# A planned attention and feed-forward kernel under another set of ranks, splits and transfer times

## Chip, core and metric

One core of a Trainium2 chip runs the kernel. The metric is device microseconds (us) for one execution, the median of several runs. Before: 872.32 us, median of 3 runs (871.31 to 877.17).

## What is computed

```python
q_pool = q.reshape(B, H, S // 2, 2, D).mean(axis=3)       # B,H,S,D = 4,8,1152,64
scores = matmul(q_pool, k.T) / sqrt(D)                    # 576 x 1152 per head
scores = scores - max(scores, axis=-1)
attn   = exp(scores) / (sum(exp(scores)) + 1e-9)
x      = matmul(attn, v)                                  # heads side by side: 2304 x 512
h      = x @ w_in                                         # 512 -> 2048
out    = (max(h, 0) + alpha * min(h, 0)) @ w_out          # 2048 -> 512
```

## The kernel before

Everything is float32; TensorE takes float32r operands (a rounded high part), and a low part is made by a subtraction, so that several products together give the precision that is wanted.

**Attention.** 32 heads run one after the other, each in stages that overlap with those of its neighbours. Preparation of head n loads the doubled transposed keys (`kk`, SP queue, L684) and the pooled queries (`qs`: for early heads two halves that are added, L680; from head 4 on a load L662 and an accumulating DMA from the GpSimd queue, L667). ScalarE makes the high parts `k1` (L694) and `q1` (L689). VectorE or GpSimd subtracts to get the low parts (keys L709, queries L722; for head 0 L806 and L796). SP copies the two halves of `k1` into `k3` (L649, two DMAs), which one pair of matmuls reads (L875) for the row maxima of the first 64 queries; the other maxima come from the pairs of L894, and VectorE reduces both from PSUM (L884, L910). The maxima are combined (L922), turned on TensorE (L928) and written by a DMA into the query operand (L944). A head then has 18 score tiles (9 key chunks, 2 query halves; matmuls L966 and L967), each followed by an exponential on ScalarE (L979) into a tile `pa`. The weighted sums with v (L1007, "AV" below) come in groups of chunks (`GROUPS`). The `pa` tiles of a head are added on VectorE or GpSimd (L992; `ADDS` names the chunks whose addition VectorE makes) into partial sums (`PARTS`: four per head before head `JH`, two from there on). For a pair of heads TensorE sums the partials over the partitions (L1029); the sums go through DRAM (`rsd` L1044, `rc` L1045, `rrd` L1050, `r` L1059), VectorE normalizes (L1066, L1078), and four DMAs store the result `xs` (L1088).

**Feed-forward.** Weights arrive as 64-bit floats and are rebuilt on VectorE and ScalarE (`wraw` L395, L398 to L419, L380, L383). Eight low sweeps (the first 5 of 16 weight blocks, during and after the last heads) and five high sweeps (the other 11) are matmuls of L471.

**Order.** A planner (`Scheduler`, lines 104 to 218) simulates five engines and the DMA queue while the program is built, and emits each operation when its simulated engine takes it. Among what can start within a slack it takes the smallest rank (`prio`), which is the head number plus or minus a constant, for example `n - KL` for the key load and `n - KS` for L709. `DF` is the fixed time in ns that it reckons for a transfer after its bytes, `D0` the same for the first loads; `TO_PE` and `FROM_PE` are its signalling times. Each engine and the SP queue then run in exactly the order written, so an SP row that waits holds back all rows behind it. Ring sizes bound how far loads run ahead (two `kk` buffers, two for pooled queries). Fillers (L1137) are matmuls on ones that keep TensorE's clock up until the simulated time `WE`; they write the PSUM bank that the AV groups use.

Of the kernel before, what the change touches and what calls it, by code (L numbers as in the profile page):

```python
# [219 lines left out]
def attention_ffn(  # L220
# [7 lines left out]
    q0: bass.AP,  # L228
    out: bass.AP,
    NLO: int = 5,  # L230
    PB: int = 14,
    QB: int = 2,
    DF: int = 1713,
    D0: int = 1171.677,
    AQ: int = 0,
    F0: float = 1.51,
    F2: float = 2.12,
    FD: tuple = (1, 1, 0),
    WE: float = 11.307,
    WG: int = 1,  # L240
    WT: float = 6.848,
    WM: int = 1,
    WB: int = 300,
    WN: int = 4,
    TO_PE: int = 164,
    FROM_PE: int = 6,
    SLP: int = 37,
    SLA: int = 171,
    SLD: int = 40,
    QL: float = -0.025,  # L250
    KL: float = 1.864,
    KR: float = 1.387,
    KS: float = -0.601,
    M0: float = 1.047,
    E0: float = 0.482,
    BD: int = 4,
    SD: tuple = (2, 16),
    LD: tuple = (0, 33),
    TD: tuple = (0, 33),
    SR: float = 0.47,  # L260
    Q0: float = -1.805,
    Q1: float = 4.468,
    GROUPS: tuple = ((3, 8), (8,)),
    PARTS: tuple = (((0, 1, 2), (3, 4), (5, 6), (7, 8)), ((0, 1, 2, 3), (4, 5, 6, 7, 8))),
    JH: int = 8,
    AB: int = 8,
    ADDS: tuple = ((2, 7, 8), (2, 7, 8)),
    PL: int = 2,
    LV: int = -9,
    LW: int = -9,  # L270
    GSB: int = 1,
    YSB: int = 4,
    R0: float = 6.415,
    R1: float = -3.03,
    R2: float = 3.013,
    R3: float = -1.183,
    W0: float = 4.578,
    W1: float = 3.204,
    W2: float = 24.069,
    W3: float = -2.969,  # L280
    YL: float = 0.328,
    MS: float = 0.123,
    EARLY: tuple = ((0, 1, 2), (3, 5), ()),
    LATE: tuple = ((0, 1, 2), (3, 5), (0, 1, 2, 3, 5)),
    SWITCH: int = 11,
    GL: float = 11.249,
    COL: float = 0.256,
    HW: float = -0.368,
    XB: int = 4,
    PT: int = 17,  # L290
    VB: int = 2,
    K1B: int = 3,
    Q1B: int = 3,
    AVB: int = 4,
# [1 line left out]
    QA: float = 1.0,  # L296
    REUSE: int = 6,
    NW: tuple = (464, 460, 460, 460, 460),
    RP: float = 32.195,
    RS: float = 0.808,  # L300
    RM: int = 31,
    RATE: float = 385.825,
):
    nc = tc.nc
# [941 lines left out]
```

## Time and profile before

| | us |
|---|---|
| median of 3 runs | 872.32 |
| the profiled execution | 870.35 |
| its span | 868.6 |
| TensorE busy | 842.8 (97%) |
| VectorE busy | 584.4 (67%) |
| ScalarE busy | 498.1 (57%) |
| GpSimd busy | 194.3 (22%) |

The page's shares are means over two unlike stages. Up to about 475 us the heads run: VectorE is busy for nine tenths of that time and TensorE has short gaps. After it the feed-forward runs, TensorE has no gap to speak of and VectorE is at a quarter for most of the time. What a change of order is worth has therefore to be read from the first stage.

### The profile page before, as it was taken

How to read it: one execution, taken by the hardware profiler on the slowest of the kernel's cores; microseconds unless marked ns; L12 is line 12 of the kernel's file. 1: busy time of each engine (PE TensorE's matmuls, PEld its weight loads, DVE VectorE, ACT ScalarE, POOL GpSimd, SP SyncE). 2: the span in 40 equal slices, each digit the busy share in tenths (PEclk: the TensorE clock that was granted, in tenths of full speed). 3: DMA queues.
4: the chain of work that ended last, by engine and by line, in shares of the span. 5: the costliest groups of instructions: out<-in, count | busy, mean ns of one | idle time of the engine just before them, and what ended most of it. 6: DMA issues, size and time to landing. Idle time of an engine off the chain costs nothing.

```text
span 868.6 us, 15141 instructions
## 1 busy us (share of the span) xinstructions
PE 842.8 (97%) x5461; PEld 713.4 (82%) x5461; DVE 584.4 (67%) x901; ACT 498.1 (57%) x1233; POOL 194.3 (22%) x149
## 2 busy tenths in 40 slices
PE   9999998999999999999999999999999999999997
PEld 7677676777777777777887999998888898988986
DVE  6898998999999988888987499932232232332322
ACT  4667787777787777867774576743223233232321
POOL 4333334445344453453541000000000000000000
PEclk9999999999999999999999999999999999999999
DMA  8637656786667556574343577647230331200301
GB/s 294 172 89 206 182 169 184 189 233 183 157 190 217 157 182 158 160 206 108 95 134 120 158 265 239 217 127 208 68 102 5 88 88 42 69 20 1 88 0 44
DMA packets 76081, 121.90 MB, mean 140 GB/s; under 512 B 21771, under 2 KB 46950, under 8 KB 76006
## 3 DMA queue, kind: packets, MB, share of 16 engines
q1 hardware_dynamic: 73990, 112.67, 42.9%
q0 software_dynamic: 2016, 8.26, 5.6%
q8 instruction: 43, 0.70, 0.3%
q14 instruction: 32, 0.26, 0.1%
HBM read 92.65 MB, written 19.02 MB: 129 GB/s over the span
## 4 chain that ended last, share of the span: by engine, by line
PE 75%; DVE 9%; DMA 8%; ACT 4%; issue 2%; SPq 0%; POOL 0%; DVEq 0%; ACTq 0%; POOLq 0%
PE bank L471 41%; PE bank L1007 13%; PE bank L966 6%; PE bank L967 5%; PE bank L894 5%; DMA k<-k 5%; PE bank L1029 2%; DVE bx L910 2%; DMA wraw<-wt 2%; ACT pa L979 2%; PE bank L875 1%; DVE pa L992 1%; DMA qs<-qt 1%; PE bank L1137 1%; DVE wbits L413 1%
## 5 line engine op out<-in xcount | busy, mean ns | idle before, releaser
L992 POOL TENSOR_TENSOR pa<-pa,pa 128x576 f32<-128x576 f32 x120 | 174.7, 1464 | 245.4 <-ACT pa L979 199.4
L979 ACT ACTIVATE pa<-bank 128x288 f32<-128x288 f32 x576 | 202.5, 407 | 29.1 <-PE bank L967 22.7
L910 DVE TENSOR_REDUCE bx<-bank 128x2 f32<-128x768 f32 x194 | 176.4, 944 | 15.7 <-PE bank L894 14.8
L966 PE MATMUL bank<-q,k 128*128 128x288 f32 x576 | 170.6, 311 | 1.3 <-ACT pa L979 1.2
L967 PE MATMUL bank<-q,k 65*128 65x288 f32 x576 | 165.1, 298 | 0.2 <-ACT q L852 0.2
L1007 PE MATMUL bank<-pa,vv 128*64 128x288 f32 x1152 | 148.5, 410 | 0.0
L1007 PEld LDWEIGHTS bank<-pa,vv 128*64 128x64 f32 x1152 | 79.1, 137 | 55.7 <-issue 6.6
L966 PEld LDWEIGHTS bank<-q,k 128*128 128x128 f32 x576 | 109.2, 190 | 10.2 <-ACT pa L979 3.8
L516 DVE TENSOR_TENSOR gw<-gs,gw 128x460 fp32r<-128x460 f32 (+1 forms) x55 | 35.1, 639 | 120.0 <-ACT gw L511 119.8
L967 PEld LDWEIGHTS bank<-q,k 65*128 65x128 f32 x576 | 109.8, 191 | 0.4 <-ACT q L852 0.4
L511 ACT ACTIVATE gw<-gs 128x460 fp32r<-128x460 f32 (+1 forms) x55 | 32.4, 589 | 125.2 <-PE bank L471 115.2
L894 PE MATMUL bank<-k,q 128*128 128x384 f32 x372 | 97.9, 345 | 3.7 <-DVE bx L910 3.4
L471 PE MATMUL bank<-wlow,wh 128*128 128x460 f32 (+1 forms) x320 | 92.9, 371 | 0.0
L471 PE MATMUL bank<-gw,wh 128*128 128x460 f32 (+1 forms) x320 | 92.8, 371 | 0.0
L505 DVE SCALAR_TENSOR_TENSOR gs<-gs,nal 128x460 f32<-128x460 f32 (+1 forms) x55 | 38.4, 699 | 52.3 <-ACT gs L500 52.3
L992 DVE TENSOR_TENSOR pa<-pa,pa 128x576 f32<-128x576 f32 x88 | 67.0, 762 | 2.3 <-POOL pa L992 2.0
L471 PE MATMUL bank<-gs,wlow 128*128 128x288 f32 x480 | 66.3, 296 | 1.3 <-ACT neg L500 1.1
L471 PE MATMUL bank<-x,wlow 128*128 128x288 f32 x480 | 67.4, 295 | 0.0
L894 PEld LDWEIGHTS bank<-k,q 128*128 128x128 f32 x372 | 60.5, 192 | 7.5 <-DVE bx L910 5.2
L471 PEld LDWEIGHTS bank<-gs,wlow 128*128 128x128 f32 x480 | 64.1, 188 | 2.5 <-ACT neg L500 1.3
L471 PEld LDWEIGHTS bank<-wlow,wh 128*128 128x128 f32 x320 | 60.1, 188 | 7.0
L471 PEld LDWEIGHTS bank<-gw,wh 128*128 128x128 f32 x320 | 60.1, 188 | 6.8
(99 smaller groups left out, 1123.4 us busy)
## 6 DMA issues: line engine op xcount, KB each, us to landing
kk<-kt SPq DMA_DIRECT2D x31, 576.0 KB
wraw<-wt SPq DMA_DIRECT2D x32, 512.0 KB
qs<-qt SPq DMA_DIRECT2D x18, 576.0 KB
vv<-vt SPq DMA_DIRECT2D x32, 288.0 KB
xs<-x SPq DMA_DIRECT2D x64, 144.0 KB
x<-xs SPq DMA_DIRECT2D x32, 288.0 KB
k<-k SPq DMA_DIRECT2D x62, 144.0 KB
qs<-qt POOLq DMA_DIRECT2D x14, 576.0 KB, 6.0
```

What stands on the lines that cost most here:

```text
L471: nc.tensor.matmul(out=ps[:, :n], lhsT=w[a, c // DMO][:, c % DMO:c % DMO + P], rhs=lo(hl), start=(first and i == 0), stop=(last and i == 2),)
L505: lambda: nc.vector.scalar_tensor_tensor(out=flat(pos), in0=flat(neg), scalar=nal[:, f:f + 1], in1=flat(pos), op0=ALU.mult, op1=ALU.add),
L511: ACT, act(n), lambda: nc.scalar.activation(out=gs.t[:, 0, :n], in_=flat(pos), func=AF.Copy),
L516: lambda: nc.vector.tensor_tensor(out=gs.t[:, 1, :n], in0=flat(pos), in1=gs.t[:, 0, :n].bitcast(F32), op=ALU.subtract),
L894: nc.tensor.matmul(out=ms.t[:, i, :JW], lhsT=(flat_of(raw, F32R) if raw else q1.t)[:, c:c + P], rhs=k1.t[:, j * JW:(j + 1) * JW], start=Tr ...
L910: lambda c=c, e=e, step=step, m=len(pair), ms=ms: nc.vector.tensor_reduce(out=bx.t.rearrange("p t j -> p (t j)")[:, c:e + 1:step], in_=ms. ...
L966: nc.tensor.matmul(out=ps.t[:, :HQ], lhsT=k1.t[:, s], rhs=q1.t[:, q], start=True, stop=False)
L967: nc.tensor.matmul(out=ps.t[:, :HQ], lhsT=k2[n % 2][:, s], rhs=q2[n % 2][:, PAD + q.start:PAD + q.stop], start=False, stop=True)
L979: lambda ps=ps, p=p, h=h: nc.scalar.activation(out=p.t[:, h], in_=ps.t[:, :HQ], func=AF.Exp, scale=SCALE),
L992: lambda a=a, b=p, part=part, e=e: e.tensor_tensor(out=part.t, in0=a.t, in1=b.t, op=ALU.add),
L1007: nc.tensor.matmul(out=av.t[h * D:(h + 1) * D, :HQ], lhsT=vv.t[:, e], rhs=p.t[:, h], start=(e == 0), stop=(e == NC - 1),)
L1029: nc.tensor.matmul(out=ps.t[g * 32:(g + 1) * 32, :HQ], lhsT=ones, rhs=acc[n + g // 2][j].t[:, g % 2], start=j == 0, stop=j == m - 1, tile_ ...
```

## The change

It changes only the planner's numbers and tables. Four partial sums per head are kept for heads 0 to 3 instead of 0 to 7 (`JH`), which also joins the AV group of those heads into one; the additions of the early heads are divided otherwise (`ADDS`); the sums of pooled queries of heads 2 and 3 (`SD`) and the two key subtractions of head 0 (`FD`) go to GpSimd; the fillers go on for longer in the plan and are 384 columns wide instead of 128 (`WE`, `WM`); rings are larger (`PB`, `AB`, `VB`); and nearly all ranks, transfer times and slacks have other values.

```diff
-    PB: int = 14,
+    PB: int = 15,
...
-    DF: int = 1713,
-    D0: int = 1171.677,
+    DF: int = 2511,
+    D0: int = 762.346,
...
-    FD: tuple = (1, 1, 0),
-    WE: float = 11.307,
+    FD: tuple = (1, 1, 1),
+    WE: float = 28.338,
...
-    WM: int = 1,
+    WM: int = 3,
...
-    TO_PE: int = 164,
-    FROM_PE: int = 6,
-    SLP: int = 37,
-    SLA: int = 171,
-    SLD: int = 40,
+    TO_PE: int = 125,
+    FROM_PE: int = 0,
+    SLP: int = 27,
+    SLA: int = 142,
+    SLD: int = 38,
...
-    KL: float = 1.864,
-    KR: float = 1.387,
-    KS: float = -0.601,
-    M0: float = 1.047,
-    E0: float = 0.482,
+    KL: float = 0.724,
+    KR: float = 1.459,
+    KS: float = -0.429,
+    M0: float = 1.043,
+    E0: float = 0.757,
...
-    SD: tuple = (2, 16),
-    LD: tuple = (0, 33),
+    SD: tuple = (4, 20),
+    LD: tuple = (1, 33),
...
-    JH: int = 8,
-    AB: int = 8,
-    ADDS: tuple = ((2, 7, 8), (2, 7, 8)),
+    JH: int = 4,
+    AB: int = 10,
+    ADDS: tuple = ((4, 5, 6, 8), (2, 7, 8)),
...
-    SWITCH: int = 11,
+    SWITCH: int = 9,
...
-    VB: int = 2,
+    VB: int = 3,
```

The order that the planner makes of it differs on every engine. Three places follow.

The SP queue from the key copies of head 19 (the first row) to those of head 20 (the last row of the first piece). Before:

```order
L649 DMA k_2872<-k_2869 64x576 x2
L684 DMA kk<-kt 128x1152
L1059 DMA r<-rrd 64x288 x4
L944 DMA q_0_108<-mm 1x5x128
L818 DMA vv<-vt 128x576
L662 DMA qs<-qt 128x1152
L395 DMA wraw<-wt 128x1024
L1088 DMA xs_74<-x_3012 64x576 x2
L1088 DMA xs_74<-x_3014 64x576 x2
L818 DMA vv<-vt 128x576
L649 DMA k_3041<-k_3017 64x576 x2
```

Now, from the key load of head 19 to the stores:

```order
L684 DMA kk<-kt 128x1152
L1045 DMA rc<-rsd 128x9
L684 DMA kk<-kt 128x1152
L1050 DMA rrd<-rc 128x9
L649 DMA k_2859<-k_2850 64x576 x2
L662 DMA qs<-qt 128x1152
L818 DMA vv<-vt 128x576
L944 DMA q_0_108<-mm 1x5x128
L395 DMA wraw<-wt 128x1024
L1059 DMA r<-rrd 64x288 x4
L649 DMA k_2999<-k_2992 64x576 x2
L1088 DMA xs_74<-x_2997 64x576 x2
```

The key copies of the even head have moved from behind the four `xs` stores and a load of v to ahead of them; the key load of head 20 has moved from behind the copies of head 19 to ahead of them, with the store `rrd` between.

VectorE at the start, where head 0's maxima are reduced (`k_0` is the low part of the keys, `bx` holds maxima). Before:

```order
L764 CAST k_159<-kk 128x384
L910 TENSOR_REDUCE bx<-bank_117 128x2
L806 TENSOR_TENSOR k_0_106<-kk,k_159 64x512
L806 TENSOR_TENSOR k_0_106<-kk,k_159 64x640
L910 TENSOR_REDUCE bx<-bank_118 128x2
```

Now these two rows stand on GpSimd, ahead of the sum and the low part of head 0's queries:

```order
L806 TENSOR_TENSOR k_0_106<-kk,k_158 64x512
L806 TENSOR_TENSOR k_0_106<-kk,k_158 64x640
L781 TENSOR_TENSOR qs<-qs 128x576
L796 TENSOR_TENSOR q_211<-qs,q_211 64x576
L680 TENSOR_TENSOR qs<-qs 128x576
```

VectorE's reductions follow each other there, and GpSimd has two more rows before the queries.

TensorE at the end of head 0 (`bank_122` is the AV bank, L928 the turn of head 1's maxima, L875 and L894 the maxima of head 2). Before:

```order
L967 MATMUL bank_120<-q_0_108,k_0_106 128x288
L928 MATMUL bank_121<-identr,mx_111 128x128
L1007 MATMUL bank_122<-pa_92,vv 64x288 x2
L1007 MATMUL bank_122<-pa_93,vv 64x288 x2
L1007 MATMUL bank_122<-pa_94,vv 64x288 x2
L1007 MATMUL bank_122<-pa_95,vv 64x288 x2
L1007 MATMUL bank_122<-pa_96,vv 64x288 x2
L894 MATMUL bank_117<-k_320,q_382 128x384 x2
```

Now:

```order
L967 MATMUL bank_119<-q_0_108,k_0_106 128x288
L1137 MATMUL bank_122<-even 128x384
L928 MATMUL bank_121<-identr,mx_111 128x128
L1137 MATMUL bank_122<-even 128x384 x9
L875 MATMUL bank_118<-k_326,bd_112 128x288 x2
L1137 MATMUL bank_122<-even 128x384 x5
L894 MATMUL bank_117<-k_313,q_357 128x384 x2
```

Fillers have taken the place of head 0's AV groups, which now follow among the scores of head 1.

## Rows read from the trace of the kernel before

**Rows 1.** Busy time by stage: stretch, its length, each engine's busy us, clock, DMA

```profile
0.00:52.85 52.85, 48.35 (x286) 37.96 (x287) 42.00 (x58) 31.53 (x75) 18.32 (x23) 0.97 0.68 205
52.85:475.63 422.78, 407.51 (x3020) 318.58 (x3018) 378.80 (x560) 315.31 (x829) 175.96 (x126) 1.00 0.61 168
475.63:868.60 392.97, 386.93 (x2159) 356.90 (x2158) 163.61 (x284) 151.29 (x330) 0.00 (x0) 1.00 0.34 102
```

**Rows 2.** TensorE's waits: us in total, times, longest

```profile
PE bank L875 <- DMA k<-k: 10.4, 8, 2.7
```

**Rows 3.** Timeline, TensorE, L875 of heads 10 and 24: start, us, idle before

```profile
147.28 0.51 PE L875 MATMUL bank<-k,bd 128*128 128x288 f32 x2 [2.66 <-DMA k<-k]
...
336.60 0.51 PE L875 MATMUL bank<-k,bd 128*128 128x288 f32 x2 [0.83 <-DMA k<-k]
```

**Rows 4.** Timeline around the key copies of head 22

```profile
300.31 1.16 ACT L694 ACTIVATE k<-kk 128x1152 fp32r<-128x1152 f32 x1
300.60 3.68 SPq L1088 DMA_DIRECT2D xs<-x  x4
...
305.00 1.11 SPq L649 DMA_DIRECT2D k<-k  x2
...
310.18 0.51 PE L875 MATMUL bank<-k,bd 128*128 128x288 f32 x2 [1.61 <-DMA k<-k]
```

**Rows 5.** Timeline around the key copies of head 23

```profile
314.83 1.16 ACT L694 ACTIVATE k<-kk 128x1152 fp32r<-128x1152 f32 x1
314.94 0.33 SPq L684 DMA_DIRECT2D kk<-kt  x1
316.01 1.16 SPq L649 DMA_DIRECT2D k<-k  x2
...
322.38 0.43 PE L875 MATMUL bank<-k,bd 128*128 128x288 f32 x2
```

**Rows 6.** Timeline, TensorE: AV groups of 4, 5, 9 chunks, partition sums

```profile
43.06 2.16 PE L1007 MATMUL bank<-pa,vv 128*64 128x288 f32 x16
...
50.27 2.65 PE L1007 MATMUL bank<-pa,vv 128*64 128x288 f32 x20
52.85 2.15 PE L1029 MATMUL bank<-pa,ones 128*32 128x288 f32 x32
...
150.34 4.59 PE L1007 MATMUL bank<-pa,vv 128*64 128x288 f32 x36
...
167.16 1.18 PE L1029 MATMUL bank<-pa,ones 128*32 128x288 f32 x16
```

**Rows 7.** Timeline at the start

```profile
7.13 1.41 DVE L806 TENSOR_TENSOR k<-kk,k 64x512 fp32r<-64x512 f32 x2
...
9.25 1.41 POOL L781 TENSOR_TENSOR qs<-qs 128x576 f32<-128x576 f32 x1 [4.84 <-DMA qs<-qt]
...
11.46 1.42 POOL L796 TENSOR_TENSOR q<-qs,q 64x576 fp32r<-64x576 f32 x1 [0.79 <-ACT q L785]
...
16.57 0.40 PE L966 MATMUL bank<-q,k 128*128 128x288 f32 x1
```

**Rows 8.** Timeline, the query transfers of heads 4 and 5, whom they hold

```profile
36.03 1.01 POOL L667 DMA_DIRECT2D qs<-qt  x1 [5.29 <-DVE bx L910]
...
45.95 0.52 ACT L640 ACTIVATE bd<-qs 64x64 fp32r<-64x64 f32 x2 [2.63 <-DMA qs<-qt]
```

**Rows 9.** Busy time of two pairs of heads, with weights and without

```profile
282.77:310.18 27.41, 25.80 (x191) 20.32 (x191) 24.57 (x36) 20.88 (x55) 12.62 (x10) 1.00 0.63 177
336.60:363.05 26.45, 25.71 (x191) 20.21 (x191) 22.75 (x33) 20.04 (x53) 12.04 (x10) 1.00 0.61 167
```

**Rows 10.** VectorE's additions: the group (count, busy, mean ns), and one

```profile
L992 DVE TENSOR_TENSOR pa<-pa,pa 128x576 f32<-128x576 f32 x88 | 67.0, 762 | 2.3 <-POOL pa L992 2.0
...
42.97 1.95 DVE L992 TENSOR_TENSOR pa<-pa,pa 128x576 f32<-128x576 f32 x1 [0.68 <-POOL pa L992]
```

**Rows 11.** Chain of waits: the landing of head 10's key copies

```profile
139.42 7.73 DMA k<-k
```

More of the change, by code (lines that the diff above doesn't have):

```diff
@@ L230, in attention_ffn @@
     NLO: int = 5,
-    PB: int = 14,
+    PB: int = 15,
     QB: int = 2,
-    DF: int = 1713,
-    D0: int = 1171.677,
+    DF: int = 2511,
+    D0: int = 762.346,
     AQ: int = 0,
-    F0: float = 1.51,
-    F2: float = 2.12,
-    FD: tuple = (1, 1, 0),
-    WE: float = 11.307,
+    F0: float = 3.972,
+    F2: float = 0.349,
+    FD: tuple = (1, 1, 1),
+    WE: float = 28.338,
     WG: int = 1,
-    WT: float = 6.848,
-    WM: int = 1,
+    WT: float = 7.765,
+    WM: int = 3,
     WB: int = 300,
     WN: int = 4,
-    TO_PE: int = 164,
-    FROM_PE: int = 6,
-    SLP: int = 37,
-    SLA: int = 171,
-    SLD: int = 40,
-    QL: float = -0.025,
-    KL: float = 1.864,
-    KR: float = 1.387,
-    KS: float = -0.601,
-    M0: float = 1.047,
-    E0: float = 0.482,
+    TO_PE: int = 125,
[3 more added lines that the diff above has]
+    SLD: int = 38,
+    QL: float = -0.025,
+    KL: float = 0.724,
[3 more added lines that the diff above has]
+    E0: float = 0.757,
     BD: int = 4,
-    SD: tuple = (2, 16),
-    LD: tuple = (0, 33),
+    SD: tuple = (4, 20),
+    LD: tuple = (1, 33),
     TD: tuple = (0, 33),
-    SR: float = 0.47,
-    Q0: float = -1.805,
-    Q1: float = 4.468,
+    SR: float = 0.422,
+    Q0: float = -3.054,
+    Q1: float = 4.61,
     GROUPS: tuple = ((3, 8), (8,)),
     PARTS: tuple = (((0, 1, 2), (3, 4), (5, 6), (7, 8)), ((0, 1, 2, 3), (4, 5, 6, 7, 8))),
-    JH: int = 8,
-    AB: int = 8,
-    ADDS: tuple = ((2, 7, 8), (2, 7, 8)),
+    JH: int = 4,
+    AB: int = 10,
+    ADDS: tuple = ((4, 5, 6, 8), (2, 7, 8)),
     PL: int = 2,
-    LV: int = -9,
-    LW: int = -9,
+    LV: int = -1,
+    LW: int = 1,
     GSB: int = 1,
     YSB: int = 4,
[L273 to L281, printed above, removed]
+    R0: float = 6.179,
+    R1: float = -3.048,
+    R2: float = 5.615,
+    R3: float = -1.627,
+    W0: float = 5.398,
+    W1: float = 3.386,
+    W2: float = 24.009,
+    W3: float = -2.562,
+    YL: float = 0.588,
     MS: float = 0.123,
@@ L284, in attention_ffn @@
     LATE: tuple = ((0, 1, 2), (3, 5), (0, 1, 2, 3, 5)),
-    SWITCH: int = 11,
-    GL: float = 11.249,
-    COL: float = 0.256,
-    HW: float = -0.368,
+    SWITCH: int = 9,
+    GL: float = 11.094,
+    COL: float = 0.122,
+    HW: float = 0.763,
     XB: int = 4,
     PT: int = 17,
-    VB: int = 2,
+    VB: int = 3,
     K1B: int = 3,
@@ L298, in attention_ffn @@
     NW: tuple = (464, 460, 460, 460, 460),
-    RP: float = 32.195,
-    RS: float = 0.808,
-    RM: int = 31,
+    RP: float = 31.323,
+    RS: float = 1.281,
+    RM: int = 30,
     RATE: float = 385.825,
```

## Prediction, made before the changed kernel ran

> **What bounds the kernel now.** I read the stages first, then TensorE's waits, then the timeline at those waits. The stages [rows 1] show two kinds of work. After 475.63 us TensorE is busy for 386.93 of 392.97 us while VectorE needs 163.61: nothing in the change touches that stage, and a new order can gain next to nothing in it. From 52.85 to 475.63 us TensorE is busy 407.51 of 422.78 us, so 15.3 us are open gaps; VectorE is busy 378.80 us, or 89.6%. Both are close to full: a gap of TensorE that is closed must be paid for by a denser VectorE.
>
> Of the 15.3 us, 10.4 us stand at one line in eight waits: the pair of matmuls L875 waits for the landing of `k3`, the copies of a head's keys [rows 2]. In the timeline the longest is head 10's with 2.66 us, head 24's is 0.83 [rows 3]; all eight belong to even heads, 10 to 28. The surroundings of one of them show why [rows 4]. For head 22 ScalarE finishes the keys at 301.47 (300.31 + 1.16), but the SP queue issues the copies at 305.00, because four `xs` stores, waiting for their data, and a load of v stand ahead; L875 then waits 1.61 us. For head 23 the copies go out at 316.01, 0.02 us after ScalarE's end at 315.99, and L875 at 322.38 does not wait [rows 5]. So this wait is made by the order of the SP queue and not by the transfer alone.
>
> **The change part by part.** The sum is made against the profiled execution, 870.35 us, which lies 1.97 below the median of the runs shown, 872.32.
>
> *Key copies.* In the new SP order the copies of even heads stand ahead of the `xs` stores, right behind the four `r` loads, which are issued long before. Head 22's would then go out at about 301.5, 3.5 us earlier, against a wait of 1.61. What is held back instead are the `xs` stores, by at most as much; they are read by low sweeps a pair or more later. One exception: for head 24 the new order still has the four stores ahead of the copies, so its 0.83 stays. Head 10 is different: its copies took 7.73 us to land [rows 11] behind a key load, a v load and a weight load; in the new queue the loads right ahead of them are the small `r`. Gain 10.4 - 0.8 = 9.6 us. Bounds: 0, if something else ends last, and 12 with the refill of the array after each gap.
>
> *Partial sums and AV groups.* Heads 4 to 7 keep two partials instead of four: two pairs whose sum on TensorE falls from 2.15 to 1.18 us [rows 6], 1.9 us. Their AV groups of 4 and 5 chunks become one of 9: 2.16 + 2.65 - 4.59 = 0.22 us each [rows 6], four times, 0.9 us. TensorE is the bound there, so both count fully: 2.8 us.
>
> *Additions.* VectorE now makes three additions in each of the heads 0 to 7 instead of two: 8 x 0.76 = 6.1 us [rows 10]. It loses the two key subtractions of head 0, 1.41 us [rows 7], and two sums of queries, of the same shape as an addition, 1.5 us. Net 3.2 us more on an engine whose cover is 52.85 - 42.00 and 422.78 - 378.80 us of idle time. Free if it falls there, 3.2 us if not; I take 1.0, since nine tenths of its time is taken.
>
> *Start.* The two subtractions go to GpSimd ahead of the queries. GpSimd took 1.42 us for 576 elements [rows 7]; by length 512 and 640 take some 2.8 us (an estimate from that row). They end at about 10.0, the query sum ends at 11.4 instead of 10.66, and the low part at 13.6 instead of 12.88: still ahead of the first score at 16.57. VectorE's chain of reductions becomes 1.41 us shorter, so the first score may come 1.4 us earlier. That is hardly kept: ScalarE waits at 45.95 for the queries of heads 4 and 5, whose accumulating DMA left GpSimd at 36.03 [rows 8], and in the new GpSimd order this DMA stands behind one addition of head 1. Against it stands that fillers now take the place of head 0's AV groups, 2.16 + 2.65 = 4.8 us of work [rows 6] that must be done later. If TensorE waits for those queries anyway, it is done in that wait. I take 0, with bounds of -1.4 and +4.8.
>
> *Key loads.* `KL` ranks them later, but with two buffers the load of head n + 2 can't go before the keys of head n are used; in the SP rows it has moved by a few places, even ahead of the odd head's copies. Nothing is taken for it, but it is a rival's cause.
>
> *Fillers.* They wait for nothing and stand in expected gaps. One stage's clock is 0.97 of full speed [rows 1], so there is up to 1.6 us to win in 52.85; I take nothing, as TensorE waits there for others.
>
> Sum: 870.35 - 9.6 - 2.8 + 1.0 + 0 = 859.0. A median lies up to 2 us above that by the runs shown; I say **860 us**. A measurement of this kernel tells about 1% from no change: below 863.6 is faster, above 881.0 slower.
>
> **The rivals.**
>
> *A, the forecast*: the waits at L875 go and no others come, 854 to 866. For it: the odd heads, which already run in the way that the even ones now should [rows 5]. Chance 0.52.
>
> *B, VectorE takes over.* The second stage would shrink to 422.78 - 12.4 = 410.4 us with 378.8 + 4.6 us of VectorE work in it (six heads' additions), 93.4% busy instead of 89.6%. If it reaches only 91.5%, the stage takes 419 us, and the kernel 866; at 90.7% nothing is gained, 870. The sign would be waits for L910 or L884 in the place of those for the copies. For it: the pair with weights takes 27.41 us with 24.57 of VectorE work, the one without 26.45 with 22.75 [rows 9], so pairs grow with VectorE's load. Against it: the new VectorE order spreads normalization and weight work over even and odd heads, where the old one had both in one. Chance 0.27.
>
> *C, more gaps close*: all 15.3 us of the stage and the 2.8, which gives 852. For it: the same spreading. Chance 0.11.
>
> *D, slower: the odd heads stall instead.* In eight of them (7 to 19 and 27) the key load of the next head, which waits for VectorE's use of the old keys, and the store `rrd` now stand directly ahead of the copies. Head 23 shows this load ahead already without harm, with 322.38 - 317.17 = 5.2 us between the second copy's issue and its use [rows 5]. From a landing of over 5.2 us on it costs; with head 10's 7.73 [rows 11] it is 2.5 us a head, 20 us in all: 879. That is slower than before. Chance 0.06, since head 10's had a weight load ahead too.
>
> *E, GpSimd and VectorE block each other.* One addition on VectorE took 1.95 us beside additions on GpSimd, where the mean of 88 is 0.762 [rows 10]. If each of the eight added ones were held for 1.2 us on the path, that is 9.6 us, and the gain is gone: 868.6. The mean says that nearly all go free. The Trainium skill (SBUF — State Buffer, Who interferes with whom) says that a VectorE instruction with two SBUF inputs contends with a GpSimd instruction that reads SBUF, and that the later one fully blocks. By that rule the trace's 1.95 us is a block; the mean says it is rare. Chance 0.04.
>
> **How the numbers follow.** 860 is A's. The range 851 to 870 takes in A, C and B up to its point of no gain; outside lie D and what is beyond these bounds. Faster by over 1%: most of A (0.43), C (0.11) and the low end of B (0.03), 0.57. Slower by over 1%: D where more than its eight heads stall, 0.05. The rest, 0.38, is within 1%.
>
> **What would show it.** Right: L875 of even heads without a wait except head 24's; copies issued within 1.2 us of the start of ScalarE's row for all heads; partition sums of 1.18 us from the third pair on; TensorE's gaps in the heads' stage down from 15 to about 6 us. Wrong: waits at L875 of odd heads (D); waits for L910 of a summed 5 us or more (B); a first pair's sum after 55 us instead of 52.85 (the start).

## The result, and the profile after

The changed kernel takes 861.6 us, the median of four runs (860.26 to 864.56); the kernel before, measured beside it, 872.88. The ratio is 0.9868, with a 95% interval of 0.9823 to 0.9912: 1.3% faster. The profiled execution took 860.93 us with a span of 859.2, 9.4 less than before.

Executions of one kernel differ, and with them TensorE's mean granted clock. In 49 fast executions of the kernel before, measured beside the experiments, the clock is 0.987 to 0.998 of full speed and the span 868.6 to 880.6 us, 873.9 in the median, and 870.7 in the median of the six with a clock of 0.997 or more. The profiled execution of the kernel before (868.6 us, 0.997) is one of the best; the four of the changed kernel have 0.997 or 0.998. The two profiles therefore compare like with like, and by the two medians of the kernel before (873.9 and 870.7) some 3 us of what separates medians can be clock.

The busy time by stage, cut at the first and the last pair's partition sum as in [rows 1] (columns: stretch, its length, busy us of PE, PEld, DVE, ACT, POOL, clock, DMA share, GB/s):

```profile
0.00:51.86 51.86, 50.02 (x292) 40.30 (x292) 43.42 (x61) 31.93 (x76) 21.60 (x25) 1.00 0.71 215
51.86:468.94 417.08, 412.28 (x3033) 324.00 (x3031) 390.45 (x566) 317.88 (x837) 181.52 (x128) 1.00 0.63 170
468.94:859.20 390.26, 383.49 (x2114) 350.10 (x2113) 159.94 (x280) 147.12 (x322) 0.00 (x0) 1.00 0.33 102
```

In the heads' stage TensorE is open for 417.08 - 412.28 = 4.8 us instead of 15.3. VectorE is busy for 390.45 us of it, 93.6%. The first stage is 1.0 us shorter and holds no stretch at a lower clock (1.00 instead of 0.97).

The heads' stage is shorter by only 5.7 us although its gaps fell by 10.5, for it holds more work: 45 more rows of L471, the feed-forward, stand ahead of the last pair's sum. Rows of L471 alone in that stage, before and now:

```profile
52.85:475.63 422.78, 20.98 (x138) 19.11 (x138) 1.00 0.61 168
```

```profile
51.86:468.94 417.08, 30.85 (x183) 26.71 (x183) 1.00 0.63 170
```

At 0.13 us from one such row to the next these are about 6 us that the feed-forward's stage no longer has to do.

TensorE's waits over the whole run (us in total, times, longest):

```profile
PE bank L966 <- ACT pa L979: 1.5, 2, 1.3
PE bank L1137 <- DVE ones L1126: 1.1, 1, 1.1
PE bank L471 <- DVE x L587: 1.0, 4, 0.3
PE bank L928 <- DVE mx L922: 0.9, 1, 0.9
PE bank L875 <- DVE bx L910: 0.8, 2, 0.4
```

The 10.4 us of L875 for the key copies [rows 2] are gone at every head. What is left at L875 are two waits of 0.4 us for VectorE's reductions (heads 3 and 7). One wait is new in the feed-forward: L471 waits for L587, VectorE's reading of a finished output.

Head 22, to be held against [rows 4]: ScalarE's key row, the SP queue behind it, and TensorE's pair:

```profile
287.01 1.15 ACT L694 ACTIVATE k<-kk 128x1152 fp32r<-128x1152 f32 x1
288.18 1.14 SPq L649 DMA_DIRECT2D k<-k  x2
290.40 2.39 SPq L1088 DMA_DIRECT2D xs<-x  x4
298.10 0.43 PE L875 MATMUL bank<-k,bd 128*128 128x288 f32 x2
```

The copies leave 1.17 us after the row starts, ahead of the `xs` stores, as forecast. That is not so at every head: for heads 24 and 28 the four stores still stand ahead, the copies leave 2.66 and 2.91 us after the row's start, and yet neither head waits. L875 also stands later: 11.1 us behind the key row, where it was 9.9 us in the kernel before, the wait of 1.61 us included. The experiments ask which of the two removed the wait, and whether the wait was the price.

### The profile page after: what moved, and what is told of

Read it like the earlier page. It is cut to its first block, busy times and chain, and to the rows that moved or that the text cites. A ratio compares the mean times of both kernels' runs of the same rounds, so it can differ in the third digit from the quotient of the medians.

```text
span 859.2 us, 15058 instructions
## 1 busy us (share of the span) xinstructions
PE 845.8 (98%) x5434; PEld 714.4 (83%) x5434; DVE 593.8 (69%) x905; ACT 496.9 (58%) x1233; POOL 203.1 (24%) x153
## 4 chain that ended last, share of the span: by engine, by line
PE 80%; DVE 10%; ACT 5%; DMA 2%; issue 2%; SPq 0%; DVEq 0%; ACTq 0%
PE bank L471 46%; PE bank L1007 11%; PE bank L966 7%; PE bank L967 6%; PE bank L894 6%; ACT pa L979 2%; DVE bx L910 2%; DVE k L709 2%; DVE pa L992 1%; DMA r<-rrd 1%; PE bank L1029 1%; PE bank L1137 1%; DVE q L722 1%; PE bank L875 1%; ACT k L694 1%
## 5 line engine op out<-in xcount | busy, mean ns | idle before, releaser
L992 POOL TENSOR_TENSOR pa<-pa,pa 128x576 f32<-128x576 f32 x120 | 181.0, 1517 | 249.6 <-ACT pa L979 215.2
L979 ACT ACTIVATE pa<-bank 128x288 f32<-128x288 f32 x576 | 203.3, 408 | 32.8 <-PE bank L967 25.4
L910 DVE TENSOR_REDUCE bx<-bank 128x2 f32<-128x768 f32 x194 | 177.2, 945 | 15.5 <-PE bank L894 14.3
L966 PE MATMUL bank<-q,k 128*128 128x288 f32 x576 | 171.2, 311 | 2.1 <-ACT pa L979 1.5
L966 PEld LDWEIGHTS bank<-q,k 128*128 128x128 f32 x576 | 108.5, 188 | 14.2 <-ACT pa L979 5.5
L894 PE MATMUL bank<-k,q 128*128 128x384 f32 x372 | 95.3, 341 | 0.1
L471 PE MATMUL bank<-gw,wh 128*128 128x460 f32 (+1 forms) x320 | 93.8, 374 | 1.5 <-DVE x L587 1.0
L471 PE MATMUL bank<-wlow,wh 128*128 128x460 f32 (+1 forms) x320 | 93.0, 371 | 0.0
L505 DVE SCALAR_TENSOR_TENSOR gs<-gs,nal 128x460 f32<-128x460 f32 (+1 forms) x55 | 38.4, 698 | 66.1 <-ACT gs L500 66.0
L992 DVE TENSOR_TENSOR pa<-pa,pa 128x576 f32<-128x576 f32 x96 | 71.2, 742 | 1.4 <-POOL pa L992 0.7
L471 PE MATMUL bank<-gs,wlow 128*128 128x288 f32 x480 | 68.4, 295 | 0.6 <-DVE gs L516 0.5
L471 PEld LDWEIGHTS bank<-gw,wh 128*128 128x128 f32 x320 | 59.3, 188 | 11.6 <-DVE x L587 5.0
L471 PE MATMUL bank<-x,wlow 128*128 128x288 f32 x480 | 68.2, 295 | 0.0
L495 ACT ACTIVATE gs<-bank 128x460 f32<-128x460 f32 (+1 forms) x55 | 30.2, 548 | 63.8 <-PE bank L471 63.8
L471 PEld LDWEIGHTS bank<-gs,wlow 128*128 128x128 f32 x480 | 65.0, 188 | 1.7 <-DVE gs L516 1.2
L471 PEld LDWEIGHTS bank<-wlow,wh 128*128 128x128 f32 x320 | 60.1, 188 | 7.0
```

The costliest lines, as they stand in the source:

```text
L471: nc.tensor.matmul(out=ps[:, :n], lhsT=w[a, c // DMO][:, c % DMO:c % DMO + P], rhs=lo(hl), start=(first and i == 0), stop=(last and i == 2),)
L495: ACT, act(n, True), lambda: nc.scalar.activation(out=flat(pos), in_=ps.t[:, :n], func=AF.Relu),
L505: lambda: nc.vector.scalar_tensor_tensor(out=flat(pos), in0=flat(neg), scalar=nal[:, f:f + 1], in1=flat(pos), op0=ALU.mult, op1=ALU.add),
L894: nc.tensor.matmul(out=ms.t[:, i, :JW], lhsT=(flat_of(raw, F32R) if raw else q1.t)[:, c:c + P], rhs=k1.t[:, j * JW:(j + 1) * JW], start=Tr ...
L910: lambda c=c, e=e, step=step, m=len(pair), ms=ms: nc.vector.tensor_reduce(out=bx.t.rearrange("p t j -> p (t j)")[:, c:e + 1:step], in_=ms. ...
L966: nc.tensor.matmul(out=ps.t[:, :HQ], lhsT=k1.t[:, s], rhs=q1.t[:, q], start=True, stop=False)
```

## The experiments

All are the kernel before or the changed kernel with one edit. "L875" is TensorE's waiting there for the key copies. "Clock" is what the half clock (the lower of TensorE's two levels, 1.2 instead of 2.4 GHz) cost up to 480 us, the sum of (1 - granted clock) x 4 us over windows of 4 us. Span, L875 and clock are those of the one profiled execution, the median and the ratio those of all. The ratio is to the kernel before, measured beside each.

| run | span | median, ratio (interval) | L875 | clock |
|---|---|---|---|---|
| before | 868.6 | 872.32 | 10.4 | 1.7 |
| changed | 859.2 | 861.6, 0.9868 (0.9823 to 0.9912) | 0 | 0 |
| e1 before, copies ahead of xs | 868.7 | 872.56, 0.9975 (0.9952 to 0.9999) | 3.0 | 5.1 |
| e2 changed, copies behind xs | 860.3 | 863.58, 0.9896 (0.9829 to 0.9963) | 0 | 0 |
| e5 before, xs further back | 880.9 | 885.02, 1.0105 (1.0053 to 1.0158) | 0.9 | 13.7 |
| e6 before, transfer time of the changed | 874.7 | 877.06, 1.0027 (0.9989 to 1.0066) | 0 | 3.4 |
| e7 changed, transfer time of before | 867.2 | 870.69, 0.9937 (0.9908 to 0.9967) | 0.4 | 1.7 |
| e11 e1, less VectorE | 880.8 | 878.97, 1.0023 (0.9997 to 1.0049) | 1.1 | 12.0 |
| e12 before, less VectorE | 879.2 | 880.65, 1.0051 (1.0015 to 1.0087) | 12.1 | 11.9 |
| e3 changed, output banks in pairs | 855.7 | 858.23, 0.9822 (0.9775 to 0.9869) | 0 | 0 |
| e4 changed, YL back | 858.5 | 859.84, 0.9835 (0.9795 to 0.9875) | 0 | 0 |
| e8 changed, no fillers | 866.1 | 865.71, 0.9887 (0.9835 to 0.9939) | 0 | 5.1 |
| e9 changed, subtractions on VectorE | 866.6 | 867.99, 0.9904 (0.9869 to 0.9939) | 0 | 3.4 |
| e10 changed, more sums | 885.6 | 887.3, 1.0138 (1.0103 to 1.0172) | 0.2 | 0 |

### The place of the key copies

Run e1 leaves the plan of the kernel before alone and only holds back the stores:

```diff
+        def emit():
+            if 10 <= n + 6 < NH and copied.get(n + 6, 0) < 2:
+                held.setdefault(n + 6, []).append(f)
+            else:
+                f()
...
-                    SP, 600,
+                    SP, 600, later(store, n),
```

> The kernel before, with the plan and the order of TensorE, VectorE, ScalarE and GpSimd as they were; only on the SP queue the four xs stores of a pair are issued behind the two key copies of the next even head instead of ahead of them (heads 10 to 28). Theory: the place of the copies in the SP queue makes the waits of L875. Then the copies of heads 12 to 28 go out within 1.2 us of ScalarE's start, the waits of L875 fall from 10.4 us to that of head 10 alone (up to 2.7 us, since v and weight loads still stand ahead of its copies), and the kernel gains 6 to 9 us, about 864. Rival 1, the landing itself under load takes too long: the waits stay above 6 us and nothing is gained (872). Rival 2, VectorE's density is the bound: the waits go but come back at L910, L884 or L922 with 5 us or more, and the gain is below 3 us.

TensorE's waits in e1 (its lines are higher by 25 here: L900 is L875, L919 is L894, L935 is L910, L962 is L937, L991 is L966, L1017 is L992):

```profile
PE bank L900 <- DMA k<-k: 3.0, 2, 2.3
PE bank L919 <- DVE bx L935: 2.7, 3, 1.7
PE bank L991 <- DVE mm L962: 2.7, 2, 1.5
```

The waits fell by 7.4 us as expected, although the copies of most even heads from 12 on left only 2.8 to 3.2 us after the start of ScalarE's row and not 1.2: a load of v still stood ahead of them. The span stayed (868.7). Two new waits for L937 came, 2.7 us, and 3.4 us more at half clock, in two stretches. The first stretch, at 149.46, follows the wait that head 10 still has at L875, 2.31 us. The place of the second new wait, on VectorE, GpSimd and TensorE, and the second stretch behind it:

```profile
265.64 1.90 DVE L419 SCALAR_TENSOR_TENSOR wmag<-wmag,wbits 128x512 f32<-128x512 f32 x1
267.46 0.27 DVE L962 TENSOR_REDUCE mm<-bank 1x64 fp32r<-1x128 f32 x1
```

```profile
265.47 1.51 POOL L1017 TENSOR_TENSOR pa<-pa,pa 128x576 f32<-128x576 f32 x1 [5.32 <-ACT pa L1004]
```

```profile
267.79 0.40 PE L991 MATMUL bank<-q,k 128*128 128x288 f32 x1 [1.50 <-DVE mm L962]
```

```profile
264.00:268.00 4.00, 2.50 (x16) 1.89 (x13) 3.97 (x6) 1.81 (x5) 1.51 (x1) 1.00 0.89 262
268.00:272.00 4.00, 3.94 (x17) 3.70 (x17) 3.44 (x5) 2.35 (x7) 1.41 (x1) 0.62 0.63 192
```

L419, a step of rebuilding the weights, usually takes 0.69 us. Here it began 0.17 us after an addition on GpSimd and ended 0.56 us after it, 1.90 us in all. L937 behind it came 1.2 us late, the scores waited 1.50 us for the bank that it reads, and then TensorE ran at half clock. The first wait for L937 has the same origin (a held L407 at 184.31). This is neither of the two rivals as I had written them: the waits came back, but from an operation that was held, not from density alone. By the medians e1 is 1.7 us faster than the kernel before (872.56 against 874.29), at the same median clock of 0.993, where 6 to 9 us were expected.

Run e2 does the reverse in the changed kernel: the copies are held until the four stores have gone, by the same kind of edit.

> The changed kernel with the orders of TensorE, VectorE, ScalarE and GpSimd as they are; only the key copies of even heads from 10 on are issued on the SP queue behind the four xs stores of the pair before, as in the kernel before. Theory: L875 waits again at most even heads, 7 to 10 us in all, and the kernel is at 867 to 871. Rival 1, the new order of the other engines gives the copies enough time even so (the stores find their data earlier): waits below 3 us and under 2 us lost (862 to 863). Rival 2: the gain of the change came from elsewhere, waits come but the time stays at 861 because they lie beside waits for VectorE.

Here the copies of head 22 leave 4.45 us after the end of ScalarE's row at 290.31, and L875 does not wait (L671 is L649 here, L900 is L875):

```profile
294.76 1.23 SPq L671 DMA_DIRECT2D k<-k  x2
```

```profile
299.94 0.43 PE L900 MATMUL bank<-k,bd 128*128 128x288 f32 x2
```

Nor does it wait for copies at any other head. That is rival 1. The span is 1.1 us longer, and the only new gap of over 0.8 us stands elsewhere, again behind a held L419:

```profile
188.71 1.89 DVE L419 SCALAR_TENSOR_TENSOR wmag<-wmag,wbits 128x512 f32<-128x512 f32 x1
```

```profile
190.85 0.40 PE L991 MATMUL bank<-q,k 128*128 128x288 f32 x1 [1.53 <-DVE mm L962]
```

So in the changed kernel the place of the copies in the SP queue is worth no more than the runs can tell apart (863.58 and 861.6 us, in separate measurements): the rest of the new order, in which L875 stands later on TensorE, covers them.

Run e5 goes on from e1, and moves the stores also behind the maxima copy L944, on the thought that the late scores were due to that copy:

```diff
-            if copied[n] == 2:
+            if copied[n] == 3:
...
+            SP, 600, first(maxima, n + 1) if n % 2 else maxima,
```

> The kernel before with its plan and the orders of the four engines; on the SP queue the xs stores of a pair now stand behind the key copies of the next even head and also behind the copy of the maxima row (L944) of the odd head, which the stores had delayed by 3.5 us in the run e1. Theory 1 (SP order was the cause, e1 lost its gain to the late maxima row): the waits of L875 stay at about 3 us, the waits for the maxima row in e1 (2.7 us) and the two stretches at half clock behind them go, and the kernel gains 6 us or more against before. Rival (the waits of L875 were slack that TensorE passes on to the next wait, with VectorE and ScalarE as close behind): waits for VectorE or ScalarE rows take their place and the gain stays below 3 us.

The thought was wrong, and the run the slowest of this group: L875 waits for 0.9 us, L966 six times for L937, 5.9 us in all. Of those waits the four that are followed by half clock (158.26, 189.52, 274.22, 304.49) each come 2.2 to 2.5 us after the start of a held weight operation (155.76, 187.35, 271.72, 302.28). The first (POOL's addition ran from 155.18 to 157.12; lines here are higher by 27 in L993, L966), and the clock around it:

```profile
155.76 1.91 DVE L407 SCALAR_TENSOR_TENSOR wbits<-wraw,wbits 128x512 int32<-128x512 int32 x1
```

```profile
158.26 0.61 PE L993 MATMUL bank<-q,k 128*128 128x288 f32 x1 [1.51 <-DVE mm L962]
```

```profile
156.00:160.00 4.00, 2.49 (x11) 2.25 (x11) 4.00 (x6) 1.95 (x5) 1.12 (x1) 0.72 0.43 147
160.00:164.00 4.00, 4.00 (x17) 4.00 (x17) 2.42 (x3) 2.31 (x7) 2.04 (x2) 0.50 0.62 221
164.00:168.00 4.00, 4.00 (x27) 3.45 (x28) 3.11 (x5) 3.69 (x12) 3.01 (x3) 0.92 0.19 16
```

A gap of 1.5 us is followed by 1.12 + 2.0 + 0.32 = 3.4 us lost at half clock. The half clock costs 12.0 us more than in the kernel before, and the span is 12.3 longer: it accounts for nearly the whole loss. The medians say the same, with smaller numbers: 9.1 us (885.02 against 875.97), at a median clock of 0.982 against 0.991, which is 8 us of 880.

### The transfer time

```diff
-    DF: int = 1713,
+    DF: int = 2511,
```

> The kernel before planned with one other number, the fixed time of a transfer, 2511 ns instead of 1713; everything else as it was. The whole plan moves. The key copies of most even heads stay behind the xs stores. Theory 1 (the planner puts L875 later in TensorE's order when it believes transfers slower): L875's waits fall below 4 us, and the kernel is at 864 to 869. Theory 2 (the SP order alone is what counts): the waits stay at 8 us or more and the time at 871 or above.

> The changed kernel planned with the fixed time of a transfer put back from 2511 to 1713 ns; everything else as changed. The key copies stand behind the xs stores again in most pairs. Theory 1 (the fitted transfer time is the part of the change that removes the waits): L875 waits 5 to 10 us, the kernel is at 866 to 870. Theory 2 (the other ranks do it): waits below 3 us and 860 to 863.

e6 is this edit to the kernel before, e7 its reverse in the changed kernel. In both runs each theory fails by half: L875 hardly waits, 0 and 0.4 us, and yet neither is faster than the kernel it is made from. By the span the two are 6.1 and 8.0 us slower; by the medians e7 is slower by 9.1 us (in separate measurements), while e6 is not told apart from the kernel before (0.9989 to 1.0066). e6 does not separate TensorE's order from the SP queue's, as it was meant to: of the even heads from 10 on, only 10, 18 and 30 have the four stores ahead of the copies in it. In e6 TensorE waits for ScalarE's exponentials instead:

```profile
PE bank L966 <- ACT pa L979: 5.5, 12, 1.1
```

From the kernel before, the waits of L875 thus go, wholly or for the most part, in three orders (e1, e5, e6), and in none of these does the time follow by more than 0.5%.

### VectorE relieved

```diff
-                    lambda a=a, b=p, part=part, e=e: e.tensor_tensor(
+                    lambda a=a, b=p, part=part, e=nc.gpsimd if c == 2 and n >= 8 else e: e.tensor_tensor(
```

> The kernel of run e1 (the kernel before with the key copies ahead of the xs stores on SP), with one of VectorE's three additions of each head from head 8 on (the one of chunk 2) issued on GpSimd instead: 24 x 0.76 = 18 us less on VectorE, 24 x 1.47 = 35 us more on GpSimd, which is then at half of the stage. Theory 1 (in e1 VectorE's late rows took over from the copies, and two stretches at half clock followed): with VectorE at 86% the waits for L937 and L910 go, L875's stay below 3 us, and the time falls to 860 to 865. Theory 2 (the gaps move on to some other row whatever is relieved): 868 or more, with waits for ScalarE, GpSimd or sums in their place.

> The kernel before, SP order and all, with only that addition of each head from head 8 on issued on GpSimd instead of VectorE. Theory 1 (L875's waits and VectorE's rows are two limits that lie one behind the other, so that taking away one of them gives nothing): the waits of L875 stay at 8 us or more and the time within 3 us of the kernel before. Theory 2 (VectorE alone was the limit): the time falls by 5 us or more although L875 still waits.

Neither was faster than the kernel before: e12 is 0.5% slower, e11 is not told apart from it (and is slower than e1, from which it is made, by 878.97 to 872.56 in separate measurements). In e12 L875 still waits, so the wait is not VectorE's doing (theory 1, in part):

```profile
PE bank L875 <- DMA k<-k: 12.1, 9, 2.0
```

The span of the profiled execution grew by 10.6 us, of which 11.9 - 1.7 = 10.2 are half clock: six stretches, where the profile of the kernel before has one, although gaps of 2.66 and 1.61 us stand in it too [rows 3, rows 4]. That is more than the edit costs: the medians differ by 4.8 us (880.65 against 875.84), and the median clock by 0.0015, about 1.3 us. In e11 waits for L979 (4.8 us), L937 (4.1) and L910 (4.0) stand in the place of L875's: theory 2. Less load on VectorE, 86.6% of the stretch from 53 to 480 us in e11, did not help.

### The wait in the feed-forward

The four output banks of a high sweep lie in two PSUM tiles of two banks each. In the changed kernel the outputs 0 and 2 share one tile, 1 and 3 the other; in the kernel before it was 0 and 3, 1 and 2. A matmul into the other half of a tile that VectorE still has to read waits for it. Run e3 turns the last group of the first high sweep round, after which the later sweeps take their banks in the old pairs:

```diff
-                    deps=[prev[m]] if prev[m] else [], prio=p + YL,
+                    deps=[prev[m]] if prev[m] else [], prio=p + YL + (0.0001 * (0, 1, 3, 2)[m] if first == 0 and f == fs[-1] else 0),
```

> The changed kernel with one thing turned: in the first high sweep's last group of output matmuls, the fourth of the four output banks is written before the third. With that the two outputs that lie in one tile of PSUM are not followed by each other with only one group between in this and the four later sweeps; in the kernel before, two groups stood between. Theory: at the ends of the five sweeps L471 waits for L587's reading of the other half of the same tile, about 0.9 us each, 3.6 us at four of them; with the turn the four waits for L587 go and the time falls by 3 to 4 us, to 858. Rival (the new rank of the output matmuls, YL, puts them too close): nothing changes here, 861 to 862, and the waits for L587 stay at four.

Run e4 leaves that and puts one rank back:

```diff
-    YL: float = 0.588,
+    YL: float = 0.328,
```

> The changed kernel with the rank offset YL of the output matmuls put back to 0.328; the plan changes only in the high sweeps, on TensorE and in a few rows of VectorE. Theory (two outputs in one tile of PSUM): the assignment of tiles stays 117, 118, 117, 118, the four waits for L587 stay, and the time stays within 1 us of the changed kernel, 861 to 862. Rival (the rank): the waits go and 3 to 4 us are won, 858.

The waits of the weight loads (PEld) from 480 us on show the kernels best. Before, where none is for L587:

```profile
PEld bank L471 <- DVE gs L516: 0.5, 2, 0.3
PEld bank L471 <- ACT gs L511: 0.3, 1, 0.3
```

Changed:

```profile
PEld bank L471 <- DVE x L587: 5.0, 9, 0.6
```

e4:

```profile
PEld bank L471 <- DVE x L587: 2.5, 5, 0.5
```

e3:

```profile
PEld bank L471 <- issue: 0.5, 1, 0.5
PEld bank L471 <- DVE gs L516: 0.2, 1, 0.2
```

In e3 no wait for L587 is left, and the span is 3.5 us shorter, 855.7, as the theory said; the pairing is the cause. In e4 five of nine are left, where I had expected all to stay: the rank has a part in it. The five high sweeps, from the first row of L471 with 464 columns to the last with 460, take 276.1 us before, 280.6 in the changed kernel, 276.9 in e3 and 278.3 in e4; so the pairing accounts for 3.7 of the 4.4 us lost, and putting the rank back alone wins 2.2 us. (e4's span is only 0.7 us shorter, for its high sweeps begin 1.6 us later.) e3 is 1.8% faster than the kernel before; against the changed kernel its median is 858.23 to 861.6, in separate measurements whose runs overlap, so there the sweeps show the gain and not the medians.

### The start

e8 takes out the 72 fillers and leaves every other row where it stood:

```diff
-            nc.tensor.matmul(
-                out=filler.t.rearrange("p (a b) -> p a b", b=P)[:, :n], lhsT=even,
...
             if sch.now < WE * 1000:
```

> The changed kernel without its 72 filler matmuls (L1137); every other row on every engine stands as it was. Theory: the fillers keep TensorE's clock up in the start; without them stretches at half clock appear in the first 50 us, the first pair's sum comes 1 to 4 us later than 51.86 us, and the kernel loses as much. Rival: TensorE waits for others there anyway; the first sum stays within 0.5 us and so does the time.

The first pair's sum came at 57.3 us instead of 51.86, 5.4 us later, beyond my range. The stretches around the drop in e8:

```profile
30.00:36.00 6.00, 3.16 (x11) 2.46 (x12) 5.68 (x8) 3.05 (x6) 0.00 (x0) 0.81 0.49 144
36.00:40.00 4.00, 4.00 (x17) 4.00 (x15) 2.07 (x4) 1.30 (x4) 1.77 (x2) 0.50 0.04 12
```

Of the 5.4 us, 3.1 are clock (0.19 x 6 + 0.5 x 4); the first score itself was 1.7 us late (17.32 against 15.59).

e9 issues the first head's two key subtractions on VectorE at the same place in the plan:

```diff
-                lambda c=c, e3=e3: e3.tensor_tensor(
+                lambda c=c: nc.vector.tensor_tensor(
```

> The changed kernel with the first head's two key subtractions (L806) issued on VectorE again, at the place in time that the plan gave them; GpSimd loses them; every other row stands as it was. Theory 1 (VectorE's chain of maxima sets the first score): 1.4 us more stand in that chain, the first score comes 1.0 to 1.4 us later than 15.59 us, and the first pair's sum up to 1 us later than 51.86. Theory 2 (the start waits for the queries of heads 4 and 5, so nothing of it is kept): the first score moves, the first sum stays within 0.3 us and the time within 1 us.

VectorE at 8.57 and TensorE at 11.57:

```profile
8.57 2.07 DVE L806 TENSOR_TENSOR k<-kk,k 64x640 fp32r<-64x640 f32 x1
```

```profile
11.57 0.91 PE L894 MATMUL bank<-k,wlow 128*128 128x384 f32 x2 [2.00 <-DVE bx L910]
```

The second subtraction met the query sum on GpSimd (8.56 to 9.97) and took 2.07 us; L894 waited 2.0 us for the reductions behind it, the clock fell (0.79 from 8 to 16 us), the first score came 3.4 us later and the first sum 3.3 us later, at 55.2. A held L419 at 244.41 cost as much again: a gap of 1.68 us and 1.7 us at half clock. So both theories had the start too small. Part of the 5.4 and the 3.3 us is the clock of these two executions, 3.4 and 1.7 us.

### The price of TensorE's work

```diff
-            for j in range(m):
+            for r, j in enumerate((0, 0, 0, 0, *range(m))):
```

> The changed kernel with 16 more matmuls in each of the 16 partition sums (the first partial's four are done five times, each time from the start, so the sum is the same): each sum is as long as it was with four partials, 2.15 us instead of 1.18. This prices TensorE's work in the heads' stage. Theory 1 (TensorE is full there, work counts at its length): 16 x 0.97 = 15.5 us more, 875 to 878. Theory 2 (VectorE's queue is as close): a part is absorbed in its waits, under 10 us more.

A sum grew by more than I had written: a matmul call of L1029 is two rows in the trace, so the edit added 32 rows to each sum, not 16. One sum in e10:

```profile
110.10 3.12 PE L1029 MATMUL bank<-pa,ones 128*32 128x288 f32 x48
```

3.12 - 1.18 = 1.94 us more, 31.0 us for 16 sums; the span grew by 26.4, or 85%. So TensorE's work in the heads' stage counts nearly at its length, and 15% fall into waits.

## Why the prediction was right, and where not

The forecast was 860 us, from 851 to 870; it is 861.6. The direction, the sign of the main terms and the size of the gaps that close were right. Two steps were not: the cause given for the main term, and the feed-forward. That the sum came so near all the same is in part luck.

*Key copies, -9.6.* The gaps of the heads' stage fell by 15.3 - 4.8 = 10.5 us, and L875 waits nowhere for the copies. But the cause I gave, that "this wait is made by the order of the SP queue", holds for the wait in the old plan and not for the time. In the old plan that order removes 7.4 us of waiting and at most 0.5% of time (e1, the interval's lower end); in the new plan L875 does not wait either way (e2). The forecast that head 24's 0.83 us would stay, since its stores stay ahead, failed for the same reason; head 28's stores stay ahead as well, which the prediction did not see, and its wait went too. By elimination what pays is the new plan as a whole, in which TensorE has other work ahead of L875. Which of its ranks does that is not shown: the one number of the heads' stage tried alone, the transfer time, takes the waits away from the kernel before and gains nothing (e6), and taken out of the changed kernel it costs 9 us without bringing them back (e7).

*Partial sums and AV groups, -2.8.* From the third pair on a sum takes 1.18 us, as forecast. By e10's 85%, measured on one profile of each kernel, it is 2.4 us, an estimate.

*Additions, +1.0.* VectorE is 93.6% busy, beyond the 91.5% at which rival B saw its limit, and TensorE's waits for L910 sum to 0.8 us. Density by itself was no limit here.

*Start, 0.* It won 1.0 us. The fillers, for which I took nothing, and the subtractions are worth 5.4 and 3.3 us in the new order (e8, e9, one profile each); the AV groups that were moved out may be what stands against them, which no run shows.

*Feed-forward.* "Nothing in the change touches that stage" is the step that failed outright. The change itself holds `YL`, the rank of the output matmuls (0.328 to 0.588), and the order ahead of the sweeps decides which bank is free first, and so which outputs share a tile. The high sweeps became 4.4 us longer, and the pairing alone cost 3.5 us of span (e3).

Sum with these: 870.35 - 10.5 - 2.4 - 1.0 + 3.5 = 859.95 against 860.93; 1.0 us is not placed. The stages' lengths give the same picture: the start is 1.0 us shorter, the heads' stage 5.7, the feed-forward 2.7; with the 6 us of L471 that moved from the third to the second put back, the heads' stage is some 11.7 us shorter and the feed-forward some 3.3 longer. So the forecast left out a loss of about 3.5 us in the feed-forward, and it reckoned the start, the additions and the gaps about 1 us each too dear; these errors cancelled.

*Rivals.* D did not come: no odd head waits at L875 for its copies. C's 852 was out of reach with the feed-forward's loss in it. E did not come in the form that I gave it, for of the 96 additions on VectorE none took more than 0.76 us; but its mechanism is there: other operations of VectorE were held, and they stand behind the two largest gaps left in the heads' stage. At the largest of them L1066 was held (1.68 us at 396.36, where 0.45 is usual), ScalarE's row behind it and the exponential came late, and the scores waited 1.26 us at 398.87. The other: L505 at 354.02 (below), then L910, L922 and L928, which waited 0.87 us.

```profile
354.02 1.75 DVE L505 SCALAR_TENSOR_TENSOR pos<-neg,nal,pos 128x288 f32<-128x288 f32 x1
355.69 0.94 DVE L910 TENSOR_REDUCE bx<-bank 128x2 f32<-128x768 f32 x1
356.67 0.17 DVE L922 TENSOR_REDUCE mx<-bx 128x4 fp32r<-128x12 f32 x1
```

```profile
356.98 0.30 PE L928 MATMUL bank<-identr,mx 128*128 128x128 f32 x1 [0.87 <-DVE mx L922]
```

## What to carry to other kernels

The sum of the waits at a line is not what their removal is worth (7.4 us of waits, 1.7 us of time in e1): take away one wait in a copy of the old order first, and see what comes late next. One profile is one execution: hold its clock against that of the other runs before explaining a difference by it. A stage that an edit does not name can still lose through what it inherits, such as which buffer is free first. In a tight order, look for single operations of VectorE that took 1 us longer than others of their line, and for gaps of TensorE that are followed by half clock, before the busy shares.

## What was not expected of the hardware

*Held operations.* In five profiles (before, changed, e1, e5, e9), 11 to 15 operations of VectorE took over 0.8 us longer than the median of their line, and every one of them overlapped an instruction of GpSimd. In the changed kernel 172 reductions from PSUM (L910) and 26 of L884 overlapped one too, and none was prolonged. The Trainium skill (SBUF — State Buffer, Who interferes with whom) has it that a VectorE instruction with two SBUF inputs contends with a GpSimd instruction that reads SBUF, that the later one is blocked, and that reductions do not contend on trn2; these rows agree. L401, which has one SBUF input, was held too, seven times in before, e1 and e5. How long a hold lasts depends on when the operation starts: in the changed kernel 29 operations with two SBUF inputs began while an addition ran on GpSimd, and 26 of them ended at the addition's end plus their own usual time less 0.13 us, within 0.06 us. Only 14 of 283 overlaps came to over 0.8 us, because most are reductions, and many others began ahead of the addition or near its end. Which operations are held changes with shifts of a few us between kernels.

*The clock after short gaps.* TensorE's granted clock fell to half at gaps of 1.2 to 2.3 us in e1, e5 and e9, and by the rows it cost 1.7 or 3.4 us each time, mostly more than the gap. In e6 it fell at 293.10, after five gaps of only 0.2 to 0.3 us in the 5 us before. It did not always fall: in the kernel before a gap of 2.66 us [rows 3] had no such stretch behind it, and the same gap at the same row cost clock in e8 and not in the changed kernel. The mean clock of the kernel before, 0.987 to 0.998 over its executions, says that it differs from one execution of the same program to the next as well. e8:

```profile
404.73 0.40 PE L966 MATMUL bank<-q,k 128*128 128x288 f32 x1 [1.27 <-ACT pa L979]
```

```profile
404.00:408.00 4.00, 3.27 (x16) 2.98 (x18) 3.97 (x8) 3.62 (x11) 1.16 (x1) 0.72 0.11 15
408.00:412.00 4.00, 4.00 (x30) 2.16 (x28) 3.25 (x4) 1.84 (x3) 1.41 (x1) 0.86 0.81 210
```

Changed:

```profile
398.87 0.40 PE L966 MATMUL bank<-q,k 128*128 128x288 f32 x1 [1.26 <-ACT pa L979]
```

```profile
396.00:400.00 4.00, 2.74 (x19) 2.42 (x18) 3.97 (x6) 3.26 (x11) 3.22 (x3) 1.00 0.00 0
400.00:404.00 4.00, 4.00 (x33) 2.64 (x33) 3.80 (x6) 3.44 (x8) 1.61 (x1) 1.00 0.56 152
```

Why it fell in one and not in the other is not shown.
